# Weight sums of the first down stage moved to later steps, and 22 output tiles finished on GpSimd instead of VectorE

## The chip, the cores and the metric

The kernel runs on one core of a Trainium2 chip. Its time is device microseconds of one launch, as the median of several runs. The core has five engines with a queue each, and they work at the same time: TensorE (PE; matmuls), VectorE (DVE), ScalarE (ACT), GpSimd (POOL) and SyncE (SP; here it only issues DMAs). Every engine goes through its own instructions in order, so an instruction that waits holds all that stand behind it on its engine. DMAs are issued from the queues of SP, ACT and POOL.

## The reference

One layer on a tensor of 2048 tokens by 1024 features in bfloat16. After a layernorm there are two branches over the same normalized tokens, and the output combines them:

```python
xn = layernorm(x)
s  = linear_attention(xn, wqkv, wo)         # 32 heads, phi(q), phi(k)
B  = (silu(xn @ w_gate) * (xn @ w_up)) @ w_down   # F = 3584
return x + s * silu(B)
```

## The kernel before, in words

**Stages.** The attention branch comes first (to about 243 us), and its result s goes to a DRAM buffer, `s_dram`. Then the second branch runs in two passes of 1024 tokens. Each has a gate/up stage (243 to 414 us and 506 to 677 us) and a down stage (414 to 506 us, the *first* one, `emit_down`; 677 us to the end, the *last* one, `emit_down_m`). TensorE never has two stages at once, but the other engines work across the borders.

**Products by sums.** All these products are done in the manner of Strassen and Winograd: sums of quarters of a matrix replace one multiplication in eight. So besides matmuls there are sums of weights, of hidden activations and of accumulators. The down stages need sums of the down weights, and the last one applies the scheme twice for its products M=1, 2, 4 and 5 (`l2_M`), whose weights are sums of sums.

**The first down stage** runs `step_a` for token tiles (0, 1) and then (2, 3) (`hf` 0 and 1; 14 blocks of the hidden dimension each, the second tile of a pair 6 steps behind the first, so 20 steps a loop), and then `step_b` for `hf` 1 and then 0. `step_a` has four matmuls for a tile and block (dx, dy and two halves of dzw), `step_b` three. Each "a" step uses one of seven weight packs "a", each "b" step one of seven packs "b" (768 KB), which SP loads into slots. After a tile's last `step_a` comes `evac_a`: ScalarE copies dx (L1289), VectorE adds dy and the two halves of dzw to it (L1290, L1291, L1295), and for `hf` 1 the next loop's `step_b` accumulates into the same PSUM tiles, so that TensorE can go on with dx when the copy is done and with dzw when L1295 is done. After a tile's last `step_b` comes `evac_b`: VectorE's L1315 (`hf` 1) or L1309 and L1310 (`hf` 0), then silu on ScalarE (L1317, L1318 or L1311, L1312), which gives three of the stage's results for each tile.

**A result** is a tile of 128 tokens by 512 columns. `fin` finishes it: multiply by s (L1221), add x (L1222), send it out (L1223, by POOL's queue in the first down stage and by SP's in the last), and then `io_load` (L1212, L1213) asks SP for x and s of a later tile. In the kernel before, both operations are VectorE's. `hold` and `io_due` postpone such loads, and `deferred` holds closures that the next gate/up stage calls, one for each key.

**Early sums.** `l2_early(M, j, store)` forms, for the "b" pack j, the four sums of sums for M=2 and for M=4 in place, on VectorE (L1136, four operations of 256 columns), and two steps later sends the weights and sums to a DRAM buffer by three DMAs of ScalarE's queue (L1128, L1129, L1130). `early(n)` calls it at step n, where n counts through the loops: 0 to 19 is `step_a` of `hf` 1, 20 to 39 is `step_b` of `hf` 1, 40 to 59 is `step_b` of `hf` 0. The numbers are

```python
for M, at, lag in ((2, lambda j: 8 + 2 * j, 2), (4, lambda j: NS + 5 + j, 2)):
```

so 8, 10, ... 20 for M=2 and 25 to 31 for M=4 (NS is 20). Between the `step_a` and `step_b` loops stands `emit_Ssum` (L712 to L715), sums of the normalized tokens for the next pass on VectorE.

**Buffers.** Three pools matter. `k2` has eight buffers of 128 x 512 float32: s1, s2, s3 of each key in the gate/up stages (L994 on ScalarE, L995 and L996 on VectorE), and c and g tiles of the down stages, g being the silu'd tile that `fin` multiplies in place. They are handed out in turn, and a new tile waits for the last reader of the one that had its buffer. `m4` has four larger buffers, `iop` five for x and s of a result. PSUM is four banks (`pps`) and two pairs (`ppd`), with `ppm` in the place of the pairs in the last stage.

**The next gate/up stage** takes its weights key by key (g, u, g, u, ...). For a key, TensorE computes yb, xb and the two halves of zw, ScalarE copies xb into s1 (L994), VectorE forms s2 and s3 (L995, L996, L1009), TensorE accumulates the remaining products onto zw, and VectorE's L1036 reads the pair, after which it can be used for the key after the next.

**The last down stage** does its products in the order 2 and 1, 7, 6, 5 and 4, 3. `flush` finishes results that wait in `fins`: four g11 tiles during product 7 (one a tile), four g22 tiles before the first tile of product 3 (`fill3`, then `out3(0)`), and g12 and g21 tiles around `out3(1)` and `out3(2)`. Two ScalarE copies (L1645) then put a partial sum into two PSUM banks, and TensorE's two last groups of matmuls (384 and 128 columns) accumulate onto it; silu and `fin` by column pieces end the kernel.

**Order.** `man.schedule` fixes the order on TensorE, VectorE, ScalarE and GpSimd as the program writes it; SP's order is written out in the second pass and the scheduler's in the first pass. 

## Time and profile before

| | |
|---|---|
| median of 3 runs | 761.97 us (761.42 to 763.3) |
| the profiled execution's own time | 762.85 us |
| its span in the profile | 761.1 us |
| granted TensorE clock, mean | 0.995 |
| TensorE busy | 744.4 us (98%) |
| VectorE busy | 592.2 us (78%) |
| ScalarE busy | 384.3 us (50%) |
| GpSimd busy | 352.2 us (46%) |
| data moved by DMA | 192.38 MB, mean 253 GB/s |

The profile is of one execution; its instructions' times are in microseconds from the span's start. A timeline row gives start, length, engine, source line, operation, output and input, and in brackets how long the engine had been idle and what released it. "ACTq" and "SPq" are the engines' DMA issues. Line numbers are those of the kernel before; in the changed kernel they are up to five higher from L1277 on.

### The profile page before, as it was taken

How to read it: one execution, taken by the hardware profiler on the slowest of the kernel's cores; microseconds unless marked ns; L12 is line 12 of the kernel's file. 1: busy time of each engine (PE TensorE's matmuls, PEld its weight loads, DVE VectorE, ACT ScalarE, POOL GpSimd, SP SyncE). 2: the span in 40 equal slices, each digit the busy share in tenths (PEclk: the TensorE clock that was granted, in tenths of full speed). 3: DMA queues.
4: the chain of work that ended last, by engine and by line, in shares of the span. 5: the costliest groups of instructions: out<-in, count | busy, mean ns of one | idle time of the engine just before them, and what ended most of it. 6: DMA issues, size and time to landing. Idle time of an engine off the chain costs nothing.

```text
span 761.1 us, 11166 instructions
## 1 busy us (share of the span) xinstructions
PE 744.4 (98%) x3835; PEld 365.9 (48%) x3899; DVE 592.2 (78%) x1119; ACT 384.3 (50%) x557; POOL 352.2 (46%) x444
## 2 busy tenths in 40 slices
PE   8999999999999999999999997999999999999997
PEld 4544544454544444444444443444444444467484
DVE  6687787886796788888889766758867777687977
ACT  5677776888956566666659201123232232323043
POOL 2444799998540276867675000021654538330000
PEclk9999999999999999999999998999999999999999
DMA  9957899879679667888799159889987885457792
GB/s 319 298 143 139 238 326 307 291 159 296 195 167 310 222 236 271 307 293 310 265 350 392 44 163 330 232 290 355 315 300 238 302 260 186 171 193 252 248 313 85
DMA packets 134426, 192.38 MB, mean 253 GB/s; under 512 B 36480, under 2 KB 108928, under 8 KB 124640
## 3 DMA queue, kind: packets, MB, share of 16 engines
q1 hardware_dynamic: 113808, 154.16, 63.6%
q0 software_dynamic: 5904, 28.58, 9.9%
q10 hardware_dynamic: 14656, 8.92, 3.9%
q8 instruction: 30, 0.49, 0.3%
q14 instruction: 28, 0.23, 0.1%
HBM read 120.85 MB, written 63.44 MB: 242 GB/s over the span
## 4 chain that ended last, share of the span: by engine, by line
PE 85%; issue 8%; DVE 4%; DMA 1%; ACT 1%; POOL 0%; SPq 0%; DVEq 0%; ACTq 0%; POOLq 0%
PE zw L967 25%; PE kv_ps L555 14%; PE xb L967 12%; PE q_ps L183 6%; PE yb L967 6%; PE dm L1499 6%; PE dm L1463 4%; PE fx L817 3%; PE s_ps L775 2%; PE dzw L1249 1%; PE kvz L577 1%; PE nd L744 1%; DMA io<-s_dram 1%; DVE g L1221 1%; PE dy L1249 1%
## 5 line engine op out<-in xcount | busy, mean ns | idle before, releaser
L967 PEld LDWEIGHTS <-w_sb 128*128 128x128 f16 (+1 forms) x1568 | 152.2, 98 | 183.9 <-issue 1.6
L967 PE MATMUL xb<-xnT,w_sb 128*128 128x512 bf16 x420 | 113.3, 379 | 1.5
L555 PE MATMUL kv_ps<-wkv_sb,xnT 128*128 128x512 bf16 x499 | 112.9, 379 | 1.3 <-ACT xnT L544 0.4
L967 PE MATMUL zw<-xnT,w_sb 128*128 128x512 bf16 x448 | 105.8, 379 | 0.8 <-DVE s L1009 0.8
L967 PE MATMUL zw<-S,w_sb 128*128 128x512 f16 x448 | 105.8, 379 | 0.0
L322 POOL TENSOR_TENSOR w_sb<-w_sb 128x512 f16<-128x512 bf16 x42 | 50.2, 1195 | 95.7 <-DVE w_sb L310 51.3
L287 ACT ACTIVATE w_sb<-w_sb 128x2048 bf16<-128x2048 bf16 x42 | 79.9, 1902 | 5.6 <-DMA w_sb<-in_B_w_up_dram 5.6
L555 PEld LDWEIGHTS <-xnT 128*128 128x128 bf16 x512 | 48.3, 98 | 56.0 <-ACT xnT L544 0.9
L1223 POOL DMA_DIRECT2D out_dram<-io x16 | 8.7, 542 | 110.9 <-DVE io L1222 110.4
L1043 ACT ACTIVATE sg<-cg 128x1024 bf16<-128x1024 f32 x28 | 29.6, 1057 | 57.4 <-DVE cg L1036 57.3
L183 PE MATMUL q_ps<-xnT,wq_sb 128*128 128x512 bf16 x249 | 58.0, 379 | 0.4
L967 PE MATMUL yb<-S,w_sb 128*128 128x512 f16 x224 | 57.4, 378 | 0.1
L995 DVE SCALAR_TENSOR_TENSOR s<-yb,rc_all,s 128x512 f32<-128x512 f32 x42 | 31.5, 749 | 29.1 <-ACT s L994 29.1
L1036 DVE SCALAR_TENSOR_TENSOR cg<-zw,rc_all,s 128x1024 f32<-128x1024 f32 x28 | 35.9, 1284 | 23.1 <-PE zw L967 12.4
L323 POOL TENSOR_TENSOR w_sb<-w_sb 128x512 f16<-128x512 bf16 x42 | 50.4, 1201 | 3.3
L325 POOL TENSOR_TENSOR w_sb<-w_sb 128x512 f16<-128x512 bf16 x42 | 50.3, 1196 | 0.0
L324 POOL TENSOR_TENSOR w_sb<-w_sb 128x512 f16<-128x512 bf16 x42 | 50.2, 1196 | 0.0
L1148 POOL TENSOR_TENSOR w_sb<-w_sb 128x512 f16<-128x512 bf16 (+3 forms) x32 | 33.1, 1055 | 36.3 <-DMA w_sb<-wd 31.8
L1249 PE MATMUL dx<-w_sb,hT 128*128 128x512 bf16 x108 | 41.9, 388 | 3.0 <-ACT s L1289 2.8
L994 ACT ACTIVATE s<-xb,rcl 128x512 f32<-128x512 f32 x14 | 9.6, 686 | 63.5 <-PE xb L967 63.5
L994 ACT ACTIVATE s<-xb,rc_all 128x512 f32<-128x512 f32 x42 | 28.3, 674 | 21.8 <-issue 12.8
L310 DVE TENSOR_SCALAR w_sb<-w_sb,cs_all 128x2048 bf16<-128x2048 bf16 x35 | 36.7, 1049 | 2.8
(230 smaller groups left out, 1326.4 us busy)
## 6 DMA issues: line engine op xcount, KB each, us to landing
w_sb<-pk_g SPq DMA_DIRECT2D x27, 1024.0 KB, 6.4
pk_g<-w_sb SPq DMA_DIRECT2D x14, 1024.0 KB, 5.1
w_sb<-pk_u SPq DMA_DIRECT2D x14, 1024.0 KB, 6.0
pk_u<-w_sb POOLq DMA_DIRECT2D x13, 1024.0 KB, 5.3
w_sb<-l SPq DMA_DIRECT2D x12, 896.0 KB, 5.0
w_sb<-in_B_w_gate_dram SPq DMA_DIRECT2D x14, 512.0 KB, 6.4
w_sb<-in_B_w_down_dram SPq DMA_DIRECT2D x28, 256.0 KB, 5.0
w_sb<-in_B_w_up_dram SPq DMA_DIRECT2D x14, 512.0 KB, 5.7
```

Source lines behind the costliest of these rows:

```text
L183: nc.tensor.matmul(q_ps[:], lhsT=wq_sb[:, dc, g * P:(g + 1) * P], rhs=xn_ap(dc, btok), start=(dc == 0), stop=(dc == DC - 1))
L287: nc.scalar.activation(out=junk, in_=raw_view(key, t), func=ACT.Square, accum_out=asum[:])
L310: nc.vector.tensor_scalar(out=w, in0=w, scalar1=cs_all[:, c:c + 1], scalar2=None, op0=ALU.mult)
L322: nc.gpsimd.tensor_tensor(out=T1, in0=b12, in1=b11, op=ALU.subtract)
L323: nc.gpsimd.tensor_tensor(out=T2, in0=b22, in1=T1, op=ALU.subtract)
L324: nc.gpsimd.tensor_tensor(out=T3, in0=b22, in1=b12, op=ALU.subtract)
L325: nc.gpsimd.tensor_tensor(out=T4, in0=b21, in1=T2, op=ALU.subtract)
L555: mm = nc.tensor.matmul(kv_ps[:], lhsT=xn_ap(dc, tok), rhs=wkv_sb[:, dc, c * CW:(c + 1) * CW], start=(dc == 0), stop=(dc == DC - 1))
L967: mm = nc.tensor.matmul(out, lhsT=lhs(k), rhs=rhs(k), start=(first and k == 0), stop=(k == HK - 1), skip_group_check=True)
L994: nc.scalar.activation(out=s1[:], in_=x_[:], func=ACT.Copy, scale=rc)
L1249: nc.tensor.matmul(out, lhsT=lhs, rhs=rhs, start=first, stop=lastk, skip_group_check=True)
L1499: nc.tensor.matmul(out, lhsT=lhs, rhs=w[:, j], start=i == 1 and j == 0, stop=j == NQ - 1, skip_group_check=True)
```

## The change

It has three parts, in the first down stage (`emit_down`), at the border to the next pass, and in the last down stage (`emit_down_m`).

First, the steps of the early sums are written out one by one. M=2: 5, 11, 14, 17, 22, 23, 24; M=4: 26, 27, 28, 29, 46, 47, 48. Stores stay two steps behind. So packs 4, 5 and 6 of M=2 come after the second `evac_a` and after `emit_Ssum`, and packs 4, 5 and 6 of M=4 after `evac_b` of the `step_b` loop for `hf` 1.

Second, the twelve results of `evac_b` in the first down stage are finished on GpSimd, arithmetic and output issue: eleven at the stage's end in one row, and the twelfth in the next gate/up stage, four keys later. (The four g22 results of `evac_a` stay on VectorE.) Loads of x and s follow other rules of `hold`, and one more pair is loaded into a buffer of `m4`.

Third, in the last down stage ten results (four g11, four g22, one g12, one g21) are finished on GpSimd, their outputs still issued by SP; the two ScalarE copies now stand ahead of the remaining results of that place on VectorE.

```diff
             fin_e = (nc.vector, nc.vector, nc.sync if last else nc.gpsimd)
+            fin_b = fin_e if last else (nc.gpsimd,) * 3
...
-                return [lambda: fin(p, t + TPB, 0, g_[:, 0, :], *fin_e),
-                        lambda: fin(p, t, 1, g_[:, 1, :], *fin_e),
-                        lambda: fin(p, t, 0, g11, *fin_e)]
+                return [lambda: fin(p, t + TPB, 0, g_[:, 0, :], *fin_b),
+                        lambda: fin(p, t, 1, g_[:, 1, :], *fin_b),
+                        lambda: fin(p, t, 0, g11, *fin_b)]
...
             def early(n):
 
-                for M, at, lag in ((2, lambda j: 8 + 2 * j, 2), (4, lambda j: NS + 5 + j, 2)):
+                for M, at in ((2, (5, 11, 14, 17, NS + 2, NS + 3, NS + 4)),
+                              (4, (NS + 6, NS + 7, NS + 8, NS + 9, 2 * NS + 6, 2 * NS + 7, 2 * NS + 8))):
                     for j in range(NQ):
-                        if n in (at(j), at(j) + lag):
-                            l2_early(M, j, n > at(j))
+                        if n in (at[j], at[j] + 2):
+                            l2_early(M, j, n > at[j])
...
                 emit_Ssum(passes[passes.index(p) + 1])
+            if not last:
+                io_load(None, m4, "m4")
...
                         if fresh and st == LEAD + 5:
                             hold[0] = False
-                            while io_due:
+                            for _ in range(5):
                                 io_due.popleft()
                                 io_load()
...
-                fins2 = evac_b(t1, fresh)
+                hold[0] = 3 if fresh else -1
+                fins += evac_b(t1, fresh)
+                if fresh:
+                    deferred.extend([lambda: None] * 4 + [fins.pop()])
                 for f in fins:
                     f()
-                    hold[0] = -1 if not fresh and not last else False
                 if fresh:
-                    deferred.extend(fins2)
-                else:
-                    for f in fins2:
-                        f()
+                    io_due.pop()
 
         def emit_down_m(p, h, base):
...
             EV = (nc.vector, nc.vector, nc.sync)
+            EP = (nc.gpsimd, nc.gpsimd, nc.sync)
...
-            def flush(n=99):
+            def flush(n=99, ev=EV):
                 while fins and n:
-                    fin(p, *fins.popleft(), *EV)
+                    fin(p, *fins.popleft(), *ev)
                     n -= 1
...
                 tt(KB[t], M7[t], KA[t])
-                flush(1)
+                flush(1, EP)
...
                     io_load(None, wgu)
-                flush()
+                flush(99, EP)
                 M3.extend(banks())
                 out3(0)
...
             go(m4_)
+            flush(2, EP)
             hs_ = [slice(0, 3 * CW // 4), slice(3 * CW // 4, CW)]
             out3(1)
-            flush(len(fins) - 1)
             ps = banks(2)
             for i in range(2):
                 nc.scalar.copy(out=ps[i][:, 0:hs_[i].stop - hs_[i].start], in_=KA[-1][:, hs_[i]])
+            flush(2)
             out3(2)
             flush()
```

## The prediction

> **What bounds the kernel now.** I read the page's shares first, then TensorE's clock by stage, then what stands in front of the one place where TensorE stops.

> ```profile
> PE 744.4 (98%) x3835; PEld 365.9 (48%) x3899; DVE 592.2 (78%) x1119; ACT 384.3 (50%) x557; POOL 352.2 (46%) x444
> ```

> TensorE is busy for 744.4 of 761.1 us, so engine time saved elsewhere counts only where TensorE waits. The windows of the two halves of step_b (columns: PE, PEld, DVE, ACT, POOL busy, granted clock, DMA share, GB/s) show the one bad place:

> ```profile
> 462.35:488.20 25.85, 21.05 (x83) 8.87 (x84) 18.70 (x53) 1.31 (x2) 1.08 (x2) 0.87 0.92 276
> 488.20:506.40 18.20, 18.09 (x85) 8.21 (x85) 5.27 (x12) 3.34 (x4) 2.70 (x5) 1.00 0.87 285
> ```

> Both halves do the same products. The first takes 25.85 - 18.20 = 7.65 us more. TensorE's timeline says how:

> ```profile
> 469.87 0.38 PE L1249 MATMUL dx<-w_sb,hT 128*128 128x512 bf16 x1 [2.82 <-ACT s L1289]
> 472.12 1.01 PE L1249 MATMUL dzw<-w_sb,hT 128*128 128x512 f16 x2 [1.87 <-DVE s L1295]
> 472.92 0.63 PE L1249 MATMUL dx<-w_sb,hT 128*128 128x512 bf16 x1
> 477.89 0.38 PE L1249 MATMUL dx<-w_sb,hT 128*128 128x512 bf16 x1
> ```

> Idle 2.82 + 1.87 = 4.69; the other 2.96 is half clock (0.63 instead of 0.38 per matmul) until 477.9. ScalarE's timeline holds the cause:

> ```profile
> 461.65 0.59 ACTq L1128 DMA_DIRECT2D l<-w_sb  x1
> 466.30 0.34 ACTq L1129 DMA_DIRECT2D l<-w_sb  x1
> 466.68 0.57 ACTq L1130 DMA_DIRECT2D l<-w_sb  x1
> 467.34 0.68 ACTq L1128 DMA_DIRECT2D l<-w_sb  x1
> 468.06 0.63 ACTq L1129 DMA_DIRECT2D l<-w_sb  x1
> 468.78 0.41 ACTq L1130 DMA_DIRECT2D l<-w_sb  x1
> 469.23 0.58 ACT L1289 COPY s<-dx 128x512 f32<-128x512 f32 x1 [8.36 <-DMA l<-w_sb]
> ```

> The copy that frees dx queues behind two stores of early sums: pack 3's (its L1129 held until 466.30, when pack 1's L1130 store, issued at 455.37, has landed at 466.28) and pack 4's. One smaller wait: 0.81 us at 514.5, where TensorE waits for VectorE, which is late by its results (L1221, L1222).

> **Early sums and stores.** Seven groups of four sums and 21 issues for each of M=2 and M=4 remain; nothing is saved, only moved. Pack 4's sums and issues leave the place before evac_a(t1); pack 3's stay, with the wait for pack 1's landing. If that landing stays at 466.3, the copy starts when pack 3's third issue is done, 466.68 + 0.57 = 467.25 instead of 469.23: 1.98 us of idleness goes. Low end 2.0 (half clock stays), high end 7.65 (the landing comes early enough, since pack 0's store goes 4 steps earlier). I take idleness 1.98 and the half clock 2.96, together 4.9: what would be left, 0.84 + 1.87, is 2.7 of 3.1 us, against 4.69 of 5.07 before.

> The clock row, 0.5 after 4.69 us of gaps, is all the trace has on the threshold. [...]

> The moved sums now queue on VectorE behind L712 to L715, four of 1.22. After L1295 (470.1 by the copy's new time) come these 4.9, seven groups of sums at 6.62/7 = 0.95 each, 6.6, and the two results left on VectorE, 1.6. So L1315 starts at 470.1 + 13.1 = 483.2 and takes 1.22. ScalarE has seven stores before its silu; the last three today, issued without waits, took 486.89 to 491.83, 1.65 each, so seven from 470.8 end at 482.4, earlier than L1315. With L1318's 1.14 GpSimd's first result can start at 484.4 + 1.14 = 485.6. Nine issues go behind evac_b, where only hf=0's evacuation (after 500) queues behind them: nothing. SP: three packs (pk_u0, pk_g1, pk_u1) wait behind the first GpSimd result's output and four behind the sixth's; their first users come after the stage's end, 10 us later than the loads' 5 to 6 us need: nothing, up to 2 if the DMA queue (0.92 busy) is late. The extra io tile only moves 0.25 MB earlier: nothing.

> **Twelve results on GpSimd, first down stage.** VectorE loses 24 operations of 0.42, 10 us. It is behind only at 514.5, so this gives 0.81. GpSimd's price for a result comes from these rows (mean ns after the bar's busy time):

> ```profile
> 532.31 4.63 POOL L1148 TENSOR_TENSOR w_sb<-w_sb 128x512 f16<-128x512 bf16 x4
> L1095 POOL TENSOR_TENSOR hs<-hs,hT 128x512 f16<-128x512 f16 x1 | 1.5, 1490 | 0.1
> 512.48 0.54 POOL L1223 DMA_DIRECT2D out_dram<-io  x1 [0.26 <-DVE io L1222]
> ```

> Two operations of 4.63/4 = 1.16, a 0.30 gap before a DMA issue (as at L1149) and 0.54 for it: 3.15 a result; beside VectorE's two-input work, 2 x 1.49 + 0.84 = 3.82. I take 3.15, since VectorE has only three groups of such sums after 486.

> What is late next: results sit in the k2 pool, eight buffers, and a buffer goes to its next tile only when its reader is done. In the changed order the s3 (L996) of the next stage's second key waits for GpSimd's ninth result, that of the third key for the eleventh. VectorE is in order: behind the second key's L996 are its L1009 and the first key's L1036, which frees the PSUM pair for TensorE's third key. That is 0.76 + 0.76 + 1.28 = 2.8 us before TensorE can go on. TensorE's timeline has that zw at 518.83 today, 11.6 us after the stage's start at 506.4 without the 0.81. The new start is 506.4 - 4.9 = 501.5, so it is due at 513.1. The ninth result ends at 485.6 + 8 x 3.15 + 2.35 = 513.15, TensorE goes on at 515.95: 2.9 us of waiting. The eleventh ends at 519.45; then L996, L1009, L1034, L1036 (3.55) give 523.0 against 515.95 + 28 matmuls x 0.216 = 522.0: 1.0. Together 3.9. Low end 0 (results that hold nobody); high end at 3.82 a result: the ninth ends at 485.6 + 8 x 3.82 + 2.98 = 519.1, 5.9 later, so 9.8.

> VectorE's two-input sums beside GpSimd's reads: 1490 against 1155 ns is what the trace shows. [...]

> **Ten results on GpSimd, last down stage.** Four g11 results at 700 to 710 lie beside work that leaves GpSimd empty: nothing. In the tail, four g22 results are ready at 740.4. Without a DMA issue (SP sends them) a result is 2.35, so six end at 740.4 + 6 x 2.35 = 754.5. The silu of out3(1)'s g12 now waits for the sixth (its buffer is g21_0's), and the two copies into PSUM queue behind it on ScalarE. Today:

> ```profile
> 750.88 0.72 ACT L1485 ACTIVATE g<-c,hsc 128x512 bf16<-128x512 f32 x1 [1.13 <-DVE c L1451]
> 751.51 0.66 ACT L1645 COPY dm<-kA 128x384 f32<-128x384 f32 x2
> ```

> New: silu 754.5 + 0.72, first copy (about half of 0.66) done at 755.6. TensorE's last two column blocks, which by their last matmul's end at 756.07 and the 3.1 us that they take start at 752.9 today, wait for it: +2.7. VectorE's backlog goes, since its 384-column L1221 started at 757.01 and its silu was done at 756.6, 0.4: together +2.3. Low end -0.4 (results that hold nobody), high end at 1.49 an operation: six take 17.9, 3.8 more, +6.1.

> **Sum.** -4.9 - 0.8 + 3.9 + 2.3 = +0.5 on the profiled execution's 762.85 (span 761.1 and 1.75 around it), 763.35. Half of the 0 to 2 for late packs adds 1: +1.5, 764.35. The median of runs is 761.97, 0.9 below the profiled one; on it the forecast is 763.5. 0.3%, 2.3 us, is what a measurement can tell here: 759.7 to 764.3 counts as the same.

> **Rivals.** A, faster: stall and half clock go whole and GpSimd holds nobody: -7.65 - 0.8 - 0.4 = -8.85 on the median, 753.1. For it: GpSimd has nothing but output issues between 479 and 532 and from 740 on. Against: 3.15 us a result beside VectorE's 0.85, and eight buffers. Halfway, the copy comes in time (first result at 482.5, stage start 498.75, third key due at 510.3) but buffers are held: TensorE goes on at 512.85, 2.5 late, so -7.65 - 0.8 + 2.5 + 1.0 + 2.3 = -2.65, 759.3. Chance of this side 0.28.

> B, slower: GpSimd's operations cost 1.49 instead of 1.16. 18 of them lie ahead of the ninth result's end and 12 ahead of the copies', so each 0.1 us an operation costs 3.0: -4.9 - 0.8 + 9.8 + 6.1 + 1 = +11.2, 773.2. It decides early: +2.3 is reached at about 1.19. For it: VectorE is busy for 13.6 to 18.7 us in such stretches. Against: in most of that one input is PSUM, and 24 rows of L1148 average 1.15 beside a busy VectorE. The slower cases lie between forecast and B; chance 0.42.

> C, the early part does not do what it says: the half clock stays, or pack 1's landing comes later, and 2.0 or less is gained. The third key is then due at 504.4 + 11.6 = 516.0, and the ninth result, which does not move, lets TensorE on at 515.95: no wait there, 1.0 for the eleventh. -2.0 - 0.8 + 1.0 + 2.3 + 1 = +1.5: the same time as the forecast, since GpSimd's ninth result caps the gain. C and the forecast's middle make up "same", 0.30.

> The forecast's own range is 760 to 767. The range that leaves two in ten out is 755.5 to 770: about 0.1 beyond it in A, 0.1 in B.

> **What would show it.** Right: the copy L1289 at about 467.3, clock 1.00 in the first half of step_b; POOL results 3.15 apart from 485; a TensorE gap of about 3 us near 513, released by VectorE's L1036, itself behind a POOL wait of L996; the tail's copies released by a POOL L1222 at about 754.5. Wrong: no POOL-released wait on either path (A); TensorE stops at 467 for over 4 us (C); POOL operations of 1.4 and more (B).

## The result, and the profile after

The changed kernel takes 771.19 us (median of 4 runs, 769.99 to 771.85) against 761.92 before: ratio 1.0117 (of the means), 95% interval 1.0098 to 1.0136. That is slower by 9.3 us, above the predicted range's end of 770. The profiled execution is the fastest of the four, 769.99 with a span of 768.2, and that of the kernel before was 0.9 above its median, so the two profiles differ by less than the medians do.

From TensorE's first matmuls in each stage, the 7.1 us of span divide up like this (duration before, after, difference):

| stretch | before | after | |
|---|---|---|---|
| to the first down stage | 414.00 | 414.12 | +0.12 |
| first down stage | 92.38 | 87.10 | -5.28 |
| next gate/up stage | 170.43 | 178.82 | +8.39 |
| last down stage, to the last matmul | 79.25 | 84.17 | +4.92 |
| from there to the end | 5.03 | 3.99 | -1.04 |

So the early part paid about what was forecast, and the two parts on GpSimd gave back more. Of the two gaps of the kernel before at 467 to 472 (2.82 and 1.87), 1.83 is left in the changed kernel, at 467 to 469. Four others have come:

```profile
510.35 1.89 PE L967 MATMUL zw<-xnT,w_sb 128*128 128x512 bf16 x8 [1.19 <-DVE s L1009]
516.00 1.11 PE L967 MATMUL xb<-xnT,w_sb 128*128 128x512 bf16 x4 [2.90 <-DVE s L995]
520.56 1.01 PE L967 MATMUL zw<-S,w_sb 128*128 128x512 f16 x2 [3.44 <-DVE cg L1036]
759.50 4.71 PE L1467 MATMUL dm<-w_sb,hT 128*128 128x384 bf16 x28 [2.90 <-ACT dm L1649]
```

Three lie at the border to the gate/up stage, one in the tail, that is, at the last column blocks. The waits of 500 to 530 us name who stands behind the first three (engine, line, what it waited for: total, times, longest):

```profile
ACT s L994 <- POOL io L1222: 9.0, 1, 9.0
DVE s L995 <- POOL io L1222: 4.2, 1, 4.2
DVE s L996 <- POOL io L1222: 3.2, 2, 1.8
```

These are s2 of the first key (sixth result), s1 of the second key (eighth) and s3 of the second and third key (ninth, eleventh): k2 buffers that GpSimd had not finished with. GpSimd's timeline gives its pace, first result, ninth and the next one:

```profile
489.02 1.15 POOL L1221 TENSOR_TENSOR g<-g,io 128x512 bf16<-128x512 bf16 x1 [10.71 <-ACT g L1319]
515.34 1.17 POOL L1221 TENSOR_TENSOR g<-g,io 128x512 bf16<-128x512 bf16 x1
518.64 1.17 POOL L1221 TENSOR_TENSOR g<-g,io 128x512 bf16<-128x512 bf16 x1
```

One result every 3.30 us, starting at 489.0. Why so late, ScalarE shows:

```profile
466.32 0.58 ACT L1290 COPY s<-dx 128x512 f32<-128x512 f32 x1 [6.71 <-DMA l<-w_sb]
474.98 0.37 ACTq L1130 DMA_DIRECT2D l<-w_sb  x1
486.70 0.41 ACTq L1130 DMA_DIRECT2D l<-w_sb  x1
487.21 0.69 ACT L1318 ACTIVATE g<-dx,hsc 128x512 bf16<-128x512 f32 x1 [17.30 <-DVE w_sb L1136]
487.80 1.14 ACT L1319 ACTIVATE g<-dd,hsc 128x1024 bf16<-128x1024 f32 x1
```

The copy that frees dx starts at 466.32 instead of 469.23. But pack 4's sums now stand behind L712 to L715 on VectorE, so the third issue of its store waits until 474.98, and the silu pair comes only after the seventh store. The windows (columns as in the prediction; the number after the instruction counts is the granted clock) show what the gaps did to the clock:

```profile
462.00:488.00 26.00, 23.82 (x110) 10.67 (x109) 19.62 (x54) 2.10 (x4) 1.08 (x2) 1.00 0.91 281
516.80:523.60 6.80, 3.36 (x10) 1.09 (x8) 3.44 (x4) 1.63 (x2) 6.01 (x7) 0.50 1.02 428
755.74:759.15 3.41, 0.86 (x4) 0.29 (x3) 3.13 (x5) 0.80 (x2) 2.50 (x3) 1.00 0.11 38
759.15:762.56 3.41, 3.06 (x10) 1.43 (x10) 3.13 (x8) 1.21 (x3) 0.00 (x0) 0.50 0.48 163
```

Full clock where it was 0.87 before, but half clock at two new places, each behind the gaps.

In the tail, ScalarE's silu that stands ahead of the two copies into PSUM waits for GpSimd's sixth result (L1222, 757.11 to 758.32), and TensorE for the first copy:

```profile
758.35 0.72 ACT L1489 ACTIVATE g<-c,hsc 128x512 bf16<-128x512 f32 x1 [3.23 <-POOL io L1222]
```

### The profile page after: what moved, and what is told of

Read it like the earlier page. It is cut to its first block, busy times and chain, and to the rows that moved or that the text cites. A ratio compares the mean times of both kernels' runs of the same rounds, so it can differ in the third digit from the quotient of the medians.

```text
span 768.2 us, 11236 instructions
## 1 busy us (share of the span) xinstructions
PE 748.0 (97%) x3899; PEld 365.9 (48%) x3899; DVE 582.5 (76%) x1075; ACT 385.0 (50%) x557; POOL 406.0 (53%) x488
## 4 chain that ended last, share of the span: by engine, by line
PE 84%; DVE 7%; POOL 3%; issue 2%; DMA 2%; ACT 1%; POOLq 0%; SPq 0%; DVEq 0%; ACTq 0%
PE zw L967 25%; PE kv_ps L555 14%; PE xb L967 12%; PE q_ps L183 6%; PE yb L967 6%; PE dzw L1249 4%; PE dm L1503 4%; PE dm L1467 3%; PE s_ps L775 2%; PE fx L817 2%; PE dx L1249 2%; POOL g L1221 2%; PE dy L1249 1%; PE kvz L577 1%; POOL io L1222 1%
## 5 line engine op out<-in xcount | busy, mean ns | idle before, releaser
L967 PE MATMUL xb<-xnT,w_sb 128*128 128x512 bf16 x448 | 115.1, 379 | 2.9 <-DVE s L995 2.9
L995 DVE SCALAR_TENSOR_TENSOR s<-yb,rc_all,s 128x512 f32<-128x512 f32 x42 | 31.4, 749 | 33.8 <-ACT s L994 29.5
L1221 POOL TENSOR_TENSOR g<-g,io 128x512 bf16<-128x512 bf16 x21 | 25.8, 1228 | 56.9 <-ACT g L1489 45.9
L1148 POOL TENSOR_TENSOR w_sb<-w_sb 128x512 f16<-128x512 bf16 (+3 forms) x32 | 33.1, 1055 | 43.0 <-DMA w_sb<-wd 42.4
L1036 DVE SCALAR_TENSOR_TENSOR cg<-zw,rc_all,s 128x1024 f32<-128x1024 f32 x28 | 35.9, 1283 | 24.9 <-PE zw L967 13.1
L994 ACT ACTIVATE s<-xb,rcl 128x512 f32<-128x512 f32 x14 | 9.6, 687 | 73.6 <-PE xb L967 64.7
L1223 POOL DMA_DIRECT2D out_dram<-io x16 | 9.2, 574 | 66.8 <-DVE io L1222 62.7
L1249 PE MATMUL dx<-w_sb,hT 128*128 128x512 bf16 x112 | 42.4, 379 | 0.0
L994 ACT ACTIVATE s<-xb,rc_all 128x512 f32<-128x512 f32 x42 | 28.3, 675 | 22.1 <-issue 12.9
```

What stands on the lines that cost most here:

```text
L967: mm = nc.tensor.matmul(out, lhsT=lhs(k), rhs=rhs(k), start=(first and k == 0), stop=(k == HK - 1), skip_group_check=True)
L994: nc.scalar.activation(out=s1[:], in_=x_[:], func=ACT.Copy, scale=rc)
L1036: nc.vector.scalar_tensor_tensor(out=d12, in0=zw[:], scalar=rc, in1=s2[:, None, :].to_broadcast([P, 2, TB]), op0=ALU.mult, op1=ALU.add)
L1221: eng1.tensor_tensor(out=y[:, cs], in0=y[:, cs], in1=io[:, 1, cs], op=ALU.mult)
L1249: nc.tensor.matmul(out, lhsT=lhs, rhs=rhs, start=first, stop=lastk, skip_group_check=True)
```

## The experiments

Theory G at the start: the border and the tail lose because GpSimd's slow results hold k2 buffers, and nothing else loses. Rivals: the moved sums and the loads of x and s (D); GpSimd's work as such, beside VectorE's (S). In the comparisons the kernel before took 761.1 to 761.3.

**Early part alone.** The kernel before with the new tuple of steps in `early` and nothing else.

> The kernel before with only the new steps of the early sums. Theory G (GpSimd's results hold k2 buffers, and nothing else loses): the next gate/up stage starts 5.2 us earlier as in the changed kernel (501.2 instead of 506.4), VectorE finishes its results in 0.85 each, and most of the 5.2 is kept: 756 to 758. Rival D (the moved sums and stores, or the loads of x and s, do the damage): the results, which start with the silu at 487 and wait for loads of x and s until 506, hold the first key as before, and 762 or more comes out.

Measured 764.12, ratio 1.0033 (1.0018 to 1.0049). Rival D's figure. The stall at 467 shrinks to 0.62 + 1.87, and at 511 TensorE waits 4.99 us: VectorE stands at L1221 for 6.25 us until x and s of a result have landed, at 511.3, with the first key's s2 and s3 behind it:

```profile
511.35 0.42 DVE L1221 TENSOR_TENSOR g<-g,io 128x512 bf16<-128x512 bf16 x1 [6.25 <-DMA io<-s_dram]
```

From TensorE's first matmuls in each stage, the first down stage is 4.4 us shorter than before (87.95), and the gate/up stage 7.3 longer (177.71).

**First down stage's results back on VectorE, all else as changed.**

```diff
-            fin_b = fin_e if last else (nc.gpsimd,) * 3
+            fin_b = fin_e
```

> The changed kernel with the twelve results of the first down stage back on VectorE (output issue by POOL as before), everything else as changed. Theory G: the three gaps at 509 to 521 and the half clock behind them go, 8.4 us between the stage's start and its third key; 771.2 - 8.4 = 762.8, with the tail's loss still in it (761 to 764). Rival D (loads held behind the first and sixth result, packs behind them): the gaps stay and 769 to 772 comes out.

Measured 771.14, ratio 1.0101 (1.0064 to 1.0138): no gain that shows in the medians (three executions took 770.9 to 771.7, the fourth 765.8). VectorE's timeline and the waits of 500 to 530 us:

```profile
511.68 0.42 DVE L1221 TENSOR_TENSOR g<-g,io 128x512 bf16<-128x512 bf16 x1 [6.22 <-DMA io<-s_dram]
```
```profile
PE zw L967 <- DVE s L1009: 8.1, 1, 8.1
```

So "nothing else loses" fell. The border has a second limit: results on VectorE wait there for x and s, which have five buffers and most of whose next loads SP issues only from 505.8 on (507.9 in the early part alone), and the next stage stands behind them in VectorE's order. GpSimd's waiting holds none of VectorE's instructions in this way; whether its buffers do is tested by the free buffers below.

**Last stage's results back on VectorE**, copies still ahead.

```diff
-            EP = (nc.gpsimd, nc.gpsimd, nc.sync)
+            EP = EV
```

> The changed kernel with the ten results of the last down stage back on VectorE, the two PSUM copies still ahead of the results behind them. Theory G: TensorE's gap of 2.90 at 756.6 and the half clock of 3.4 us behind it go, 4.5 us at the last matmul; VectorE's backlog of results at the end returns, about 1: 771.2 - 3.5 = 767.7 (766.5 to 768.5). If the tail's loss is not GpSimd's: 771.

Measured 765.08, ratio 1.0038 (1.0020 to 1.0057): 0.79 points, about 6.0 us, below the changed kernel, more than the 3.5 expected; no gap remains in the tail. Between the two profiled executions it is 4.9: the last stage is 4.9 shorter to its last matmul (79.26), and the backlog of 1 that was expected at the end did not return (4.09 from the last matmul to the end, against 3.99 changed and 5.03 before). So the end's gain of about 1 comes from the new order of copies and results, not from GpSimd. The other 1.1 of the 6.0 is a difference between executions that the profiles do not show.

**Last stage alone** on the kernel before (only the third part of the change).

> The kernel before with only the last stage changed (ten results on GpSimd, copies ahead). Theory G: TensorE waits 2.9 us for the first copy, behind the sixth GpSimd result, with half clock after it in most runs; 761.2 + 2.9 + 0 to 1.7 - 1.0 = 763.1 to 764.8. If the tail costs only together with the border (its phase or its queue): 761.

Measured 764.88, ratio 1.0049 (1.0029 to 1.0070), +3.6: the tail loses by itself. Its profiled execution has the gap, 2.91 at 752.8, without half clock.

**Free buffers.** Every result still on GpSimd, but the silu tiles of `evac_b` (except two g11) and c11 lie in parts of the two kept tiles that are free by then.

```diff
-                g_ = k2([P, 2, CW], BF16, "g12")
-                g11 = k2([P, CW], BF16, "g11")[:]
                 if fresh:
                     s1, s34 = kept[t]
-                    c11 = k2([P, CW], FP32, "c11")[:]
+                    c11 = s1
+                    g_ = s34[:, 0, :].bitcast(BF16).rearrange("p (q n) -> p q n", q=2)
+                    g11 = s34[:, 1, :].bitcast(BF16)[:, 0:CW] if t == 0 else \
+                        x_spare[0][:, 3, :].bitcast(BF16)[:, CW:2 * CW]
+                elif not last:
+                    g_ = x_spare[t - 2][:, 3, :].bitcast(BF16).rearrange("p (q n) -> p q n", q=2)
+                    g11 = k2([P, CW], BF16, "g11")[:]
...
```

> The changed kernel with every result still on GpSimd, but the silu tiles of the first down stage's evac_b (except two g11) kept in free parts of the two kept tiles instead of k2 buffers. So no L994, L995 or L996 of the first two keys waits for GpSimd, and the third key's waits for the third and the sixth result alone. Theory G (the buffers' holding, not GpSimd's time as such): TensorE's gaps at 509 to 521 go although GpSimd works until 525, 8.4 us: 762.8 (761 to 764). [...]

Measured 759.60, ratio 0.9983 (0.9962 to 1.0005), 11.6 us or 1.3 points below the changed kernel and better than the range expected. Its border window:

```profile
498.00:530.00 32.00, 31.84 (x147) 14.56 (x149) 22.35 (x27) 10.74 (x15) 21.78 (x23) 1.00 0.88 325
```

TensorE is busy for 31.84 of 32 us at full clock while GpSimd works for 21.8 of them, at the same 3.30 a result. GpSimd's slowness and its company with VectorE cost TensorE nothing here; holding the buffers did. In the profiled executions the gate/up stage takes 169.21 instead of 178.82, 9.6 us less, and 170.43 before. That is what the buffers are worth. The first down stage is 2.5 shorter, too, mostly since a store landed earlier (see the early part in the next section), and the tail has its gap of 2.9 without half clock; neither is the work of the buffers.

**Free buffers, and the last stage on VectorE** (both edits above).

> The kernel with free buffers (the first down stage's twelve results on GpSimd, their silu tiles out of the k2 pool) and the last stage's ten results on VectorE. Theory G: neither gaps at the border nor the copies' wait at the tail; against the free-buffer kernel (759.6 beside 761.2 of before) the tail gives 2.9 of gap and, on some runs, up to 1.7 of half clock, less 1 of backlog: 756.5 (755.5 to 757.5). If the tail's wait were hidden by something else, 759 to 760.

Measured 753.59, ratio 0.9900 (0.9868 to 0.9933): 7.7 us faster than the kernel before, and the fastest of all. Neither border nor tail has a gap over 0.5.

**The same with the old early steps.**

> Free buffers and the last stage on VectorE (753.6 with the new early steps), but the early sums at their old steps. It gives the worth of the early part where nothing holds the border. Theory G: the whole stall of 7.65 comes back, less what the clock's phase gives: 759.5 to 761.5. If the early part is worth little by itself, 755 or less.

Measured 759.00, ratio 0.9976 (0.9962 to 0.9989), just under the range expected. The early part is worth 0.76 points, 5.8 us, once nothing at the border takes it back; in the profiled executions the first down stage takes 91.18 instead of 86.86, and the gate/up stage the same 169.21.

**The border part with old early steps** (the changed kernel, old tuple, last stage on VectorE).

> The border part alone: twelve results on GpSimd with buffers in k2, but the early sums at their old steps and the last stage's results on VectorE. Theory G: the stall at 467 stays (stage start 506.4), the first result can start with the silu at 493.6, the sixth ends at 493.6 + 5 x 3.3 + 2.4 = 512.5, the eighth at 519.1, the ninth at 522.4, so the third key's zw comes at 525.2 instead of 518.83: +6.4 and up to 1.7 of half clock, 767.5 to 769.5. Rival (the border only loses because the early part brought its start forward): 761 to 762.

Measured 770.04, ratio 1.0121 (1.0101 to 1.0142): the border part loses without the early part, too. First result and the third key's zw:

```profile
494.84 1.15 POOL L1221 TENSOR_TENSOR g<-g,io 128x512 bf16<-128x512 bf16 x1 [13.72 <-ACT g L1319]
```
```profile
526.40 2.96 PE L967 MATMUL zw<-S,w_sb 128*128 128x512 f16 x7 [3.02 <-DVE cg L1036]
```

That zw comes 7.6 us after the 518.83 of before, where 6.4 was expected: GpSimd started 1.2 later.

**M=4's first four sums and stores later**, to start GpSimd's row earlier.

```diff
-                              (4, (NS + 6, NS + 7, NS + 8, NS + 9, 2 * NS + 6, 2 * NS + 7, 2 * NS + 8))):
+                              (4, (2 * NS, 2 * NS + 1, 2 * NS + 2, 2 * NS + 3, 2 * NS + 6, 2 * NS + 7, 2 * NS + 8))):
```

> The changed kernel with the first four sums and stores of M=4 moved on as well, from steps 26 to 29 to steps 40 to 43, so that ScalarE's first silu of evac_b stands behind nine issues instead of 21. Buffers as in the changed kernel. Theory G with the start of GpSimd's row as what decides: first result at about 481 instead of 489, the sixth at 500, the ninth at 510, so the waits at 509 and 513 go and the one at 517 shrinks to 1 or less; with the half clock 6 to 8 us less than the changed kernel: 763.5 to 765.5, the tail's loss still in it. Rival (GpSimd's length, not its start, or weight packs that now come late because their slots are freed 9 us later): 769 or more.

Measured 770.76, ratio 1.0124 (1.0092 to 1.0156): no gain. The first result does start at 478.7, but the stores now stand in front of the next evacuation on ScalarE:

```profile
506.25 1.15 ACT L1312 ACTIVATE g<-dd,hsc 128x1024 bf16<-128x1024 f32 x1 [23.13 <-DMA l<-w_sb]
```
```profile
510.28 1.86 PE L967 MATMUL xb<-xnT,w_sb 128*128 128x512 bf16 x4 [3.80 <-ACT s L994]
```

The queue moved from one silu to the next one. The same edit in the fastest kernel:

> Free buffers, M=4's first four sums and stores at steps 40 to 43, and the last stage's results on VectorE. Theory G: no wait is left at the border for the later stores to take away, so no difference from the kernel with free buffers and the last stage on VectorE: 756.5, 755 to 758. Rival (late slots): 759 or more.

Measured 762.79, ratio 1.0029 (1.0009 to 1.0049): 9.2 us lost. In the profiled executions 6.2 of it lie in the gate/up stage (175.37 against 169.21), again by ScalarE, whose L1320 comes at 509.9 with a TensorE gap of 3.14 and half clock behind it (1.81 for four matmuls of 1.03 before the gap). Another 2.3 lie in the first down stage, ahead of the steps that were moved: a store landed later there (see the early part in the next section). Both expectations missed the wait; the rival's reason (late packs) is not what the traces show either.

**Outputs issued by SP**, so that a result takes GpSimd less (last stage on VectorE).

```diff
-            fin_b = fin_e if last else (nc.gpsimd,) * 3
+            fin_b = fin_e if last else (nc.gpsimd, nc.gpsimd, nc.sync)
```

> The changed kernel with the last stage's results on VectorE (765.1), and the outputs of the twelve GpSimd results issued by SP instead of GpSimd; buffers in k2 as in the change. A result then takes GpSimd 2.4 instead of 3.3. Theory G, pace times the eight buffers: first result at 489, sixth done at 503.4, eighth at 508.2, ninth at 510.6, before the first, second and third key need them: the gaps at 508 to 520 shrink to 1 or less and 757 to 759 comes out. Rival (SP, in order, holds its weight packs and loads behind each output): 763 or more, with TensorE waiting for weights or VectorE for loads.

Measured 769.13, ratio 1.0116 (1.0096 to 1.0135): the rival. The pace becomes 2.34 as expected, six results end at 503.2, and then:

```profile
513.68 1.15 POOL L1221 TENSOR_TENSOR g<-g,io 128x512 bf16<-128x512 bf16 x1 [10.51 <-DMA io<-in_A_x_dram]
```

SP, in order, had waited for results ahead of each output (14.4 us in six waits), with the next loads behind them, and the seventh and later results kept their buffers for 10.5 us more.

**The g11 results on GpSimd in the fastest kernel.**

> Free buffers and VectorE in the tail, with the four g11 results during product 7 on GpSimd as in the change. These were costed at nothing: 753.6, within 1 either way. If they hold product 7's or product 5's tiles: 755 or more.

Measured 756.57, ratio 0.9927 (0.9898 to 0.9955). Inconclusive: the medians differ by 3.0, but in the profiled executions 1.7 of the 2.6 us between the two last matmuls arise in the first down stage (88.58 against 86.86), where the kernels are the same; the last stage differs by 0.4 (79.67 against 79.26).

## Why the prediction was wrong

The forecast was 763.5 with slower as likeliest sign (0.42); the time lies 1.2 above the range. The path was named rightly: buffers held by GpSimd's ninth result at the border, the copies behind the sixth in the tail. The step that failed is the border's sum, above all the start of GpSimd's row and the half clock that it left out behind its own gaps; a smaller one is the tail's half clock.

**Right, in part by luck: the early part.** Copy at 466.32 (467.25 forecast), idleness left at this place 1.83 (2.7 forecast), half clock gone; -5.28 against -4.9. The sum held pack 3's store, which waits for a landing, until 466.3; it went on at 465.5, so that only the second wait was left. The change alone does not set this time: with the same early steps the store goes on at 461.4 in the free-buffer kernel, where no gap at all is left and this stage takes 84.61, and at 466.1 in the free-buffer kernel with M=4 later. That one has the 2.7 of the forecast, 0.81 + 1.87, and it lost the clock (0.50 from 469.61 to 473.03):

```profile
469.84 1.01 PE L1249 MATMUL dzw<-w_sb,hT 128*128 128x512 f16 x2 [1.87 <-DVE s L1296]
```

So in the changed kernel the half clock went with 1.83 us of idleness, after a copy earlier than forecast. That it goes at the 2.7 that the sum assumed was the author's estimate, which no run shows; here it stayed.

**Right in kind, wrong in size: the border.** Forecast -0.8 + 3.9 = +3.1, measured +8.39. TensorE goes on with the third key at 520.56 instead of 515.95: the 2.9 of waiting became 7.53, in three gaps. The 1.0 for the eleventh result did not come, but 1.5 of half clock did.
- The first result's start, 485.6 forecast, was 489.0. The step "seven from 470.8 end at 482.4" took the pace of stores that had no sums to wait for; with L1130 held until 474.98 they ended at 487.1. The same paragraph had put pack 4's sums behind 4.9 us of L712 to L715 on VectorE; it did not make their store wait for them.
- The price of a result: 3.15 forecast, 3.30 measured, since two dependent operations stand 1.22 to 1.25 apart and the issue takes 0.58. Eight of them add 1.2. So the ninth result ended at 517.7 instead of 513.15, and with all shifted by 4 us the sixth and the eighth, which the sum did not follow up at all, became late as well (1.19 and 2.90).
- Half clock behind the new gaps has no term in the sum. The zw group behind them took 3.39 instead of 1.89.

The 1 us for late weight packs did not come either: no wait of TensorE for a pack is among the changed kernel's.

**Right in its gap, wrong in its sequel: the tail.** Gap 2.90 against 2.7 forecast, at the line and by the copy named. But half clock followed, and the last 28 matmuls took 4.71 (3.22 in the free-buffer kernel, at full clock). +3.9 with the end's gain of 1.04, against +2.3. About 0.5 of it is neither gap nor clock; the four g11 results, put at nothing, added 0.4 to this stage in the profiled execution of the kernel that has them alone (79.67 against 79.26).

**Rivals.** B's size came true without B's mechanism on TensorE's path: at the border and ahead of the copies GpSimd's operations took 1.15 to 1.25, not 1.49; the high end was right for a reason that it did not have. But B's price exists in the changed kernel. Six of the eight operations of the g11 results took 1.48 to 1.60, and the sums on VectorE beside them, whose inputs both lie in SBUF, took two and a half times as long as in the kernel before (first row before, the others changed):

```profile
701.77 4.29 DVE L1451 TENSOR_TENSOR hT<-hT 128x1024 f16<-128x1024 f16 x7
705.00 10.92 DVE L1455 TENSOR_TENSOR hT<-hT 128x1024 f16<-128x1024 f16 x7
705.97 1.60 POOL L1221 TENSOR_TENSOR g<-g,io 128x512 bf16<-128x512 bf16 x1
```

TensorE has no gap there, so this cost it nothing at that place. At the border VectorE's sums take one input from PSUM; its rows (0.75 for L995 to L1009) and GpSimd's (1.15 to 1.17) kept their times. The row of 1.49 from which B's price came (L1095 at 408.94 in the kernel before) had no VectorE sum with both inputs in SBUF beside it: L1078, with one tensor as input, took 1.65 there (0.75 in its other four) and ended at 409.42, and L995 and L996 behind it, with one input in PSUM, took 0.74 and 0.75. What slows the two engines in these places, the runs do not show.

C's remark that the ninth result caps what the early part gains held: in the k2 kernels the early part is worth 0.83 points (1.0121 against 1.0038) only because the same part also moves GpSimd's start, from 494.8 to 488.3 in the two kernels compared. Rival A assumed that without held buffers the early gain is simply kept. With results on GpSimd and buffers free, that is so (759.6, and 753.6 without the tail; A's figure was 753.1). With results on VectorE it is not (764.1): the stall at 467 had covered VectorE's wait for loads, and this the prediction had not asked. Results on VectorE with free buffers were not run.

## What to carry to other kernels

Work given to a slower engine (here two operations of 1.15 to 1.17 us each on GpSimd, of 0.42 on VectorE) holds its operands for as long as that engine takes, so count the buffers in the pool ahead of each new tile before counting the engine's time; here the stage behind the same work took 178.8 or 169.2 us, depending on where its tiles lay. When a stall is removed, list all waits that end inside or just behind it (loads and stores too), as they are late next. An order that moves a queue of DMA issues from in front of one instruction moves it in front of the next on that engine, and it pays only if that one can wait: here the silus of `evac_b` could once their buffers were free, and the next evacuation could not (TensorE waited 3.80 and 3.14 us for it).

## What the runs showed of the hardware

```profile
742.35:745.76 3.41, 1.82 (x9) 0.71 (x8) 2.22 (x3) 0.32 (x1) 3.33 (x3) 1.00 0.14 46
745.76:749.17 3.41, 2.12 (x14) 1.27 (x14) 3.31 (x9) 2.01 (x4) 0.11 (x1) 1.00 0.34 115
```

Neither is idle for more than 1.6 us, and the clock stays at 1.00 (the stretches' edges are counted back from that execution's own clock change at its end). The half-clock periods of the kernel before and the changed one lasted 6.83 us (470.91 to 477.74 and 516.80 to 523.63) and 3.41 (759.15 to 762.56). The stretches at full clock in which TensorE was idle for up to 1.77 us kept it there (762.56 to 765.98 in the changed kernel), and those with 2.55 or more lost it (755.74 to 759.15, and 2.61 at 513.39 to 516.80, in the changed kernel; 3.03 at 467.50 to 470.91 before). Two other traces lie between these: 1.87 idle kept it (the kernel with g11 results on GpSimd, 468.06 to 471.48; mean clock of that execution 1.0), and 2.22 lost it (free buffers with M=4 later, 756.33 to 759.75; mean clock 0.994). So for the two gaps of 2.9 us, what differed was how each lay across these stretches: 2.55 us of idleness in one, or no more than 1.6 in either. Executions of one kernel differ by some us along with their clock: of ten of the free-buffer kernel, the five with a mean clock of 0.998 and more took 756.0 to 758.8, the five below it 760.4 to 762.5.
